# Layer one's gMLP first half, last two token chunks: block pairs as seven half products

## The chip, the cores and the metric

The kernel runs on one core of one Trainium2 chip. The metric is the device time of one execution in microseconds (us), and the numbers given are medians of several executions.

The engines have short names in the text: PE is the matrix engine (TensorE), DVE is VectorE, ACT is ScalarE, POOL is GpSimd, and SP is SyncE, which only issues transfers (DMAs). Each engine takes its instructions in the order in which the program lists them; an instruction that waits holds up all that stand behind it on that engine.

## The reference

Two layers, each made of an attention block with a linear kernel and a gMLP block, over 2048 tokens of 512 features, in 32-bit floats:

```python
for layer in range(2):
    x = x + attention(layernorm(x), wqkv, wo)      # 32 heads of 16, phi(t) = elu(t) + 1
    z = gelu(layernorm(x) @ w_in)                  # 2048 x 1792
    z1 = z[:, :896]; z2 = layernorm(z[:, 896:])
    g = w_sp @ z2 + b_sp[:, None]                  # over the tokens: 2048 x 2048
    x = x + (z1 * g) @ w_out
```

The change concerns `z1 = gelu(layernorm(x) @ w_in[:, :896])` of the first of the two layers. The kernel calls the layers L = 0 and L = 1, so "layer one" is L = 0.

## The kernel before

Every 32-bit operand of a product is split into a high part h (rounded to the matrix engine's format) and a low part l, and a product is three matmuls, h·h, h·l and l·h (`mm3`, L227). An ACT copy makes h (L214) and a DVE subtraction makes l (L217).

The tokens are cut into 16 tiles of 128 (i) and 4 chunks of 512 (n), the 896 features of z1 into 7 blocks of 128 (f). For each layer the phases are P1 (keys and queries), a transition, P2 (attention output, both gMLP input products) and P4 (the product over the tokens, the gate and the output product).

P2 of layer L = 0 is `P2.run`, a loop over token steps s = 1 to 18. The order within a step is written out by hand, and each engine's queue is in that order; nothing is scheduled afterwards. A step between 6 and 15 holds, for different tiles at once:

- `b(s)`: the turned attention input of tile s is read back from a scratch tensor (qt), turned on DVE (L448) and split (ACT L214, DVE L217).
- `c(s-1)`: the attention output product of tile s-1, 12 matmuls of 512 columns. `c2` adds it to x on DVE (L907) and takes mean and variance (L359, L361 on DVE; L363, L364, L366 on POOL). `c3` normalises on ACT (L372), stores x, and stores the tile through a scratch tensor (yt) so that it can be read back turned.
- `d(s-2)`: tile s-2 comes back from yt, is turned on DVE (L448) and split (ACT L214, DVE L217) into its 128 columns of xT[n].
- `e4(s-4)`: the last layernorm of z2 for tile s-4, on ACT (L372).
- `e(s-3)`: the z2 product of tile s-3, 24 matmuls of 448 columns, into two banks; `e2` is its gelu on ACT (L1068), `e3` its statistics on DVE and POOL.
- twice `f()`: one block (n, f) of z1 for one chunk, 12 matmuls of 512 columns; `fout` is its gelu on ACT (L1135) and its store (tensor z). Blocks are queued as soon as a chunk's four tiles are done, at the end of steps 5, 9, 13 and 17.
- `sums.tick()`: sums of the weights of the later product over the tokens (POOL L1604, loads and stores on SP).

Fourteen of the 28 blocks are thus worked off up to step 13 and nine more in steps 14 to 18; the five that are left when the loop ends run in `P4.run`, in the `while p2.f()` loop, beside the splits for P4's first products.

Layer L = 1 already computes chunks 2 and 3 by blocks 0 to 2 and 3 to 5 as seven products (`first_a`, `first_b`, `T1`, `T2`, `tail`). `first_a(f)` does half a product into bank u, and ACT copies u to bank y (L1170); `first_b(f)` then adds the other half to u itself. In layer L = 1 other work stands between the two (`odd`, L1190 and on). The weight sums that this needs are made in the P1 phase of L = 1 from the raw weights, on POOL (`FSums.sums`), split on ACT and DVE, and stored to a scratch tensor (w1s).

PSUM has 8 banks; a bank is free again when its reader on ACT or DVE is done.

Of the kernel before, what the change touches and what calls it, by code (L numbers as in the profile page):

```python
# [15 lines left out]
P = 128  # L16
# [95 lines left out]
WADD = {2: 0, 4: 1, 6: 2}  # L112
# [40 lines left out]
def mixer_kernel(ctx: ExitStack, tc: tile.TileContext, x_in, wqkv, wo_d, win1_d, win2_d, wsp_d, bsp_d, wout_d,  # L153
# [299 lines left out]
    class P1:  # L453
# [185 lines left out]
        def run(self, sums):  # L639
            side = deque([self.win2] * NF)  # L640
            ND = NT - DEFER
            for s in range(1, NT + 2):
# [54 lines left out]
                if self.L:  # L697
                    if 9 <= s < NT + 1:
                        sums.halve(28 + (s - 9) // 2, None, (s - 9) % 2)
                    if s in WADD:  # L700
                        if not WADD[s]:
                            self.fsums = FSums()
                        self.fsums.load(WADD[s])
                    if s - 1 in WADD:
                        self.fsums.sums(WADD[s - 1])
                    if s - 2 in WADD:
                        self.fsums.split(WADD[s - 2])
                        if WADD[s - 2] == 2:
                            self.fsums.close()
# [15 lines left out]
    class FSums:  # L725


        def __init__(self):
            self.raw = quads.get([P, 2, 2, 512])
            self.parts = quads.get([P, 2, 2, 512], F32R)  # L730

        def load(self, f):
            for k in range(2):
                nc.sync.dma_start(self.raw[:, f % 2, k], win1_d[f + 3 * k])

        def sums(self, f):
            p, q = (self.raw[:, f % 2, k].rearrange("p (k n) -> p k n", k=2) for k in range(2))
            for o, a, b, op in ((q[:, 1], q[:, 0], q[:, 1], OP.add), (q[:, 0], p[:, 0], q[:, 0], OP.subtract),
                                (p[:, 0], q[:, 1], p[:, 0], OP.subtract), (p[:, 1], p[:, 1], p[:, 0], OP.subtract)):
                nc.gpsimd.tensor_tensor(o, a, b, op=op)  # L740

        def split(self, f):
            p, q = (self.raw[:, f % 2, k].rearrange("p (k n) -> p k n", k=2) for k in range(2))
            for m in range(2):
                h, l = (self.parts[:, m, k] for k in range(2))
# [4 lines left out]
                for k in range(2):  # L750
                    nc.sync.dma_start(w1sums[f, m][k], self.parts[:, m, k].bitcast(F32))

        def close(self):
            quads.put(self.raw, self.parts)
# [72 lines left out]
    class P2:  # L827
        def __init__(self, p1):
# [4 lines left out]
            self.wf = deque([w1parts[f] for f in list(range(NF)) * 2 + [0, 6, 1, 2, 6]]  # L833
# [107 lines left out]
        def d_low(self, i):  # L941
# [9 lines left out]
            if k == 3:  # L951
                self.fnext = [(n, f) for f in (range(NF) if n < 2 or not self.L else (NF - 1,))]
# [226 lines left out]
        def first_out(self, *fs):  # L1179
            for f in fs:  # L1180
                if f:
                    self.wfetch()
# [1229 lines left out]
```

## Time and profile before

| | |
|---|---|
| median of 3 runs | 1346.25 us (1345.23 to 1347.37) |
| span of the profiled execution | 1345.0 us, from its first instruction to its last |
| its own time | recorded as the span alone; the fastest of the runs lies 0.2 us above it, the median 1.25 us |
| mean granted TensorE clock | 0.999 |
| PE busy | 1338.2 us, 99% of the span |
| DVE, ACT, POOL busy | 1043.7, 726.6, 462.6 us (78%, 54%, 34%) |
| HBM read and written | 204.08 and 101.71 MB |

PE's busy time comes from matmuls whose ends are modelled, so a matmul of 512 columns shows some 389 ns while the next one starts after some 227. Durations on PE are therefore taken from start to start. A row of a timeline gives start, duration, engine, line, what it writes and reads, how many instructions are merged into it, and in brackets how long the engine idled before it and for what.

### The profile page before, as it was taken

How to read it: one execution, taken by the hardware profiler on the slowest of the kernel's cores; microseconds unless marked ns; L12 is line 12 of the kernel's file. 1: busy time of each engine (PE TensorE's matmuls, PEld its weight loads, DVE VectorE, ACT ScalarE, POOL GpSimd, SP SyncE). 2: the span in 40 equal slices, each digit the busy share in tenths (PEclk: the TensorE clock that was granted, in tenths of full speed). 3: DMA queues.
4: the chain of work that ended last, by engine and by line, in shares of the span. 5: the costliest groups of instructions: out<-in, count | busy, mean ns of one | idle time of the engine just before them, and what ended most of it. 6: DMA issues, size and time to landing. Idle time of an engine off the chain costs nothing.

```text
span 1345.0 us, 19202 instructions
## 1 busy us (share of the span) xinstructions
PE 1338.2 (99%) x6538; PEld 1141.4 (85%) x6538; DVE 1043.7 (78%) x1662; ACT 726.6 (54%) x1219; POOL 462.6 (34%) x613
## 2 busy tenths in 40 slices
PE   9999999999999999999999999999999999999998
PEld 7888888888888888889988888888888888888898
DVE  7679877763797789888867777778689858899885
ACT  5774534334643264445677755557677433666454
POOL 3755675544022300301425543544531012121021
PEclk9999999999999999999999999999999999999999
DMA  5897477877877986884867652678777445579343
GB/s 184 279 318 272 164 262 254 293 270 258 298 236 256 285 265 203 293 306 80 179 172 230 173 133 89 208 238 272 217 206 231 168 168 178 177 241 313 122 79 64
DMA packets 172403, 290.30 MB, mean 216 GB/s; under 512 B 14480, under 2 KB 53904, under 8 KB 172048
## 3 DMA queue, kind: packets, MB, share of 16 engines
q1 hardware_dynamic: 154192, 251.58, 55.5%
q0 software_dynamic: 18112, 37.49, 13.0%
q8 instruction: 51, 0.84, 0.2%
q14 instruction: 48, 0.39, 0.1%
HBM read 204.08 MB, written 101.71 MB: 227 GB/s over the span
## 4 chain that ended last, share of the span: by engine, by line
PE 96%; DMA 1%; DVE 1%; ACT 1%; SPq 0%; issue 0%; POOL 0%; DVEq 0%
PE bank L228 14%; PE bank L230 14%; PE bank L229 13%; PE bank L1920 12%; PE bank L1921 12%; PE bank L1922 12%; PE bank L2118 3%; PE bank L2119 3%; PE bank L2120 3%; PE bank L986 1%; PE bank L988 1%; PE bank L987 1%; DMA pg<-yt 1%; PE bank L384 1%; PE bank L2132 1%; PE bank L2131 1%
## 5 line engine op out<-in xcount | busy, mean ns | idle before, releaser
L1921 PE MATMUL bank<-qd,pg 128*128 128x512 f32 x736 | 286.5, 389 | 0.0
L1920 PE MATMUL bank<-qd,pg 128*128 128x512 f32 x736 | 286.4, 389 | 0.0
L1922 PE MATMUL bank<-qd,pg 128*128 128x512 f32 x736 | 286.3, 389 | 0.0
L1695 ACT ACTIVATE qd<-qd 128x1024 fp32r<-128x1024 f32 x142 | 149.4, 1053 | 127.3 <-PE bank L1922 107.0
L1698 DVE TENSOR_TENSOR qd<-qd,qd 128x1024 fp32r<-128x1024 f32 x132 | 169.2, 1284 | 52.6 <-ACT qd L1695 41.7
L230 PE MATMUL bank<-qd,pg 128*128 128x512 f32 x448 | 174.6, 390 | 0.0
L1921 PEld LDWEIGHTS bank<-qd,pg 128*128 128x128 f32 x736 | 138.2, 188 | 28.9 <-DVE qd L1698 0.3
L1920 PEld LDWEIGHTS bank<-qd,pg 128*128 128x128 f32 x736 | 138.2, 188 | 28.7 <-DVE bg L1870 0.2
L1922 PEld LDWEIGHTS bank<-qd,pg 128*128 128x128 f32 x736 | 138.2, 188 | 28.7
L228 PE MATMUL bank<-qd,pg 128*128 128x512 f32 x308 | 120.6, 392 | 0.3 <-DVE pg L217 0.3
L1961 POOL TENSOR_TENSOR bg<-bg,pg 128x512 f32<-128x512 f32 x28 | 45.7, 1632 | 218.1 <-ACT qd L1695 99.4
L229 PE MATMUL bank<-qd,pg 128*128 128x512 f32 x308 | 120.1, 390 | 0.0
L230 PEld LDWEIGHTS bank<-qd,pg 128*128 128x128 f32 x448 | 84.1, 188 | 17.8 <-DVE pg L217 0.2
L363 POOL TENSOR_SCALAR rs<-mv 128x1 f32<-128x1 f32 x80 | 25.1, 314 | 190.0 <-DVE mv L361 181.0
L372 ACT ACTIVATE pg<-pg,nb,rs 128x512 f32<-128x512 f32 x52 | 42.2, 812 | 85.5 <-POOL nb L366 79.3
L1604 POOL TENSOR_TENSOR pg<-pg,pg 128x512 f32<-128x512 f32 x48 | 68.0, 1417 | 59.2 <-DMA pg<-in_wsp_dram 57.3
L214 ACT ACTIVATE pg<-pg 128x512 fp32r<-128x512 f32 x85 | 53.0, 624 | 61.7 <-DVE pg L1789 18.4
L2120 PE MATMUL bank<-wo,qd 128*128 128x256 f32 x288 | 81.4, 283 | 0.0
L2118 PE MATMUL bank<-wo,qd 128*128 128x256 f32 x276 | 78.2, 283 | 0.0
L2119 PE MATMUL bank<-wo,qd 128*128 128x256 f32 x276 | 78.0, 283 | 0.0
L228 PEld LDWEIGHTS bank<-qd,pg 128*128 128x128 f32 x308 | 57.9, 188 | 12.5 <-DVE pg L217 0.7
L229 PEld LDWEIGHTS bank<-qd,pg 128*128 128x128 f32 x308 | 58.0, 188 | 12.1 <-DVE qd L217 0.2
(276 smaller groups left out, 3278.6 us busy)
## 6 DMA issues: line engine op xcount, KB each, us to landing
qd<-s SPq DMA_DIRECT2D x62, 512.0 KB, 4.2
qd<-in_wsp_dram SPq DMA_DIRECT2D x40, 512.0 KB, 4.1
qd<-hP SPq DMA_DIRECT2D x40, 512.0 KB, 4.7
pg<-z SPq DMA_DIRECT2D x56, 256.0 KB, 4.9
pg<-in_wsp_dram SPq DMA_DIRECT2D x52, 256.0 KB, 4.3
s<-pg SPq DMA_DIRECT2D x48, 256.0 KB, 3.7
z<-pg SPq DMA_DIRECT2D x40, 256.0 KB, 3.3
pg<-w POOLq DMA_DIRECT2D x38, 256.0 KB, 4.6
```

The source lines that it names most:

```text
L228: nc.tensor.matmul(out, ah, bh, start=start, stop=False)
L229: nc.tensor.matmul(out, ah, bl, start=False, stop=False)
L230: nc.tensor.matmul(out, al, bh, start=False, stop=stop)
L1604: nc.gpsimd.tensor_tensor(t, a, b, op=OP.add)
L1695: self.mark = nc.scalar.activation(w[:, 0], r, AF.Copy)
L1698: nc.vector.tensor_sub(w[:, 1], r, w[:, 0].bitcast(F32))
L1920: m(out, h[:, o], w[:, 0, j, :], start=start, stop=False, skip_group_check=True)
L1921: m(out, h[:, o], w[:, 1, j, :], start=False, stop=False, skip_group_check=True)
L1922: m(out, l[:, o], w[:, 0, j, :], start=False, stop=stop, skip_group_check=True)
L2118: m(out, A, x, start=start and f == 0, stop=False, skip_group_check=True)
L2119: m(out, A, y, start=False, stop=False, skip_group_check=True)
L2120: m(out, B, x, start=False, stop=stop and f == 2, skip_group_check=True)
```

## The change

Layer L = 0 gets the same scheme for chunks 2 and 3, blocks 0 to 5; block 6 of both chunks, and chunks 0 and 1, stay as they were. For a pair of blocks (f, f+3) and the two chunks, four blocks of 12 matmuls become seven products of 6.

- In the loop, `FONE` says how many plain blocks a step does: 2 in steps 6, 7, 8 and 10, 11, 12, and 1 in steps 9, 13 and 14, none later. Steps 15, 16 and 17 each end with `first_a(f)`, `first_b(f)` and `first_out(f)` for f = 0, 1, 2, directly one behind the other.
- The weight sums move from L = 1's P1 to these token steps. Steps 13, 14 and 15 load two raw weight tiles each (SP); steps 14, 15 and 16 make four sums (now on DVE, 128x256 each), four high parts (ACT) and four low parts (DVE), and store four tiles of 256 KB (SP). The stores also serve L = 1, whose POOL sums, loads and stores go.
- Step 16 ends with `raw(0)` (DVE, 128x1024). Step 17 gets `T1` (two DVE subtractions of 128x1024), `T1split` (ACT and DVE, 128x1024) and `raw(1)`, right behind `d(15)` and ahead of `e4` and `e2`. Step 18 gets `T2`, eight DVE operations of 128x512, and two weight loads on POOL's queue.
- The loop over the five remaining blocks in `P4.run` is replaced by `tail()` for both layers: one plain block and the other five products of each pair, 102 matmuls, with the splits of P4's first products at three places in it.
- From tile 5 on, normalised and turned tiles live in the z tiles in place of pages.

PE loses 18 matmuls (6400 rows become 6382), DVE and ACT gain rows, and SP loses eight.

The diff, cut to its core:

```diff
+FONE = {6: 2, 7: 2, 8: 2, 9: 1, 10: 2, 11: 2, 12: 2, 13: 1, 14: 1}
-WADD = {2: 0, 4: 1, 6: 2}
+WADD = {13: 0, 14: 1, 15: 2}
...
         def load(self, f):
-            for k in range(2):
-                nc.sync.dma_start(self.raw[:, f % 2, k], win1_d[f + 3 * k])
+            self.raw[f] = [load(win1_d[f + 3 * k]) for k in range(2)]
...
         def split(self, f):
+            raw = self.raw.pop(f)
+            p, q = (t.rearrange("p (k n) -> p k n", k=2) for t in raw)
+            V = nc.vector
+            V.tensor_add(q[:, 1], q[:, 0], q[:, 1])
+            V.tensor_sub(q[:, 0], p[:, 0], q[:, 0])
+            V.tensor_sub(p[:, 0], q[:, 1], p[:, 0])
+            V.tensor_sub(p[:, 1], p[:, 1], p[:, 0])
             for m in range(2):
-                h, l = (self.parts[:, m, k] for k in range(2))
+                h, l = pages.get(PAGE, F32R), pages.get(PAGE, F32R)
                 for k, s in enumerate((q[:, 1 - m], p[:, m])):
                     high(h[:, 256 * k:256 * k + 256], s)
                 for k, s in enumerate((q[:, 1 - m], p[:, m])):
                     low(l[:, 256 * k:256 * k + 256], s, h[:, 256 * k:256 * k + 256])
...
+                if s == NT + 1:
+                    self.T1()
+                    self.T1split()
+                    self.raw(1)
+                if s == NT + 2:
+                    quads.put(*self.xT.pop(2))
+                    self.T2()
+                    self.wfetch()
+                    self.wfetch()
                 if s >= 4:
                     self.e4(s - 4)
                 self.xturn.load(s - 1)
                 if s >= 3:
                     self.e(s - 3)
                     self.e2(s - 3)
                     self.e3(s - 3)
-                self.f()
-                self.f()
+                for _ in range(FONE.get(s, 0)):
+                    self.f()
+                if s in (15, 16, 17):
+                    self.first_a(s - 15)
+                    self.first_b(s - 15)
+                    self.first_out(s - 15)
+                if s in WADD:
+                    if not WADD[s]:
+                        self.fsums = FSums()
+                    self.fsums.load(WADD[s])
+                if s - 1 in WADD:
+                    self.fsums.split(WADD[s - 1])
...
-            while p2.f():
-                self.zahead(min(self.zmade, 3))
+            for _ in p2.tail():
+                n += 1
+                if n == 1:
+                    self.sums.store()
+                self.zahead(n - 1)
+                self.sp(n - 1)
+                if n < 3:
+                    self.fetch(n + 3)
             self.zahead(3)
-            if p2.win1 is not None:
-                p2.win1.free()
```

Three places in the queues. The words in brackets name whose count an instruction waits for (a DMA queue, an engine); lines 200 to 700 move by one in the changed kernel, later ones by others.

ACT around step 15, before. The rows are the split for b(15), the normalisation of tile 14, the split for d(13), e4(11), the two gelus of e(12), and the gelus of two plain blocks:

```order
L214 ACTIVATE pg_351_3365<-pg_350_3363 128x512 [waits DMAHW7_49,DVE_49]
L372 ACTIVATE pg_353_3393<-pg_327_3115,nb,rs 128x4x4x32 [waits DVE_49,DMAHW3_49,Activation_49,Pool_49]
L214 ACTIVATE qd_16_3275<-pg_354_3397 128x4x128 [waits DVE_49]
L372 ACTIVATE z_z_3308<-z_z_3308,nb,rs 128x896 [waits Activation_49]
L1068 ACTIVATE z_z_3430<-bank_127_3404 128x448 [waits PE_49]
L1068 ACTIVATE z_z_3430<-bank_128_3417 128x448 [waits PE_49]
L1135 ACTIVATE pg_356_3456<-bank_129_3443 128x512 [waits DMAHW5_49,PE_49,Activation_49]
L1135 ACTIVATE pg_357_3473<-bank_130_3460 128x512 [waits DMAHW6_49,PE_49,Activation_49]
```

ACT at the same place in the changed kernel, from the four high parts of the first weight sums on:

```order
L215 ACTIVATE pg_324_3350<-pg_312_3225 128x256 [waits DMAHW3_49,DMAHW2_49,DVE_49]
L215 ACTIVATE pg_324_3350<-pg_311_3223 128x256 [waits DMAHW1_49,DVE_49]
L215 ACTIVATE pg_326_3358<-pg_312_3225 128x256 [waits DMAHW7_49]
L215 ACTIVATE pg_326_3358<-pg_311_3223 128x256 [waits DVE_49]
L215 ACTIVATE z_q<-pg_329_3374 128x512 [waits DVE_49]
L373 ACTIVATE z_y<-pg_305_3115,nb,rs 128x4x4x32 [waits DVE_49,Activation_49,Pool_49]
L215 ACTIVATE qd_16_3279<-z_y 128x4x128 [waits DVE_49]
L373 ACTIVATE z_z_3312<-z_z_3312,nb,rs 128x896 [waits Activation_49]
L1059 ACTIVATE z_z_3441<-bank_126_3415 128x448 [waits PE_49]
L1059 ACTIVATE z_z_3441<-bank_127_3428 128x448 [waits PE_49]
L1161 ACTIVATE bank_128_3454<-bank_129_3455 128x512 [waits PE_49]
L1134 ACTIVATE pg_332_3469<-bank_129_3455 128x512 [waits PE_49,Activation_49]
```

Four high parts have come ahead of step 15's own rows, and behind the gelus of e(12) the copy of u to y (L1161) stands before the gelu of u.

PE at the end of step 15 in the changed kernel (the last three rows of `first_a(0)`, the first of `first_b(0)` and what follows it):

```order
L1144 MATMUL bank_129_3455<-qd_14_2753,bg_5_1763 128x512
L1145 MATMUL bank_129_3455<-qd_15_2754,bg_5_1763 128x512
L1146 MATMUL bank_129_3455<-qd_14_2753,bg_6_1764 128x512
L1144 MATMUL bank_129_3455<-qd_14_2753,bg_5_1763 128x512 [waits Activation_49]
L1145 MATMUL bank_129_3455<-qd_15_2754,bg_5_1763 128x512
L1146 MATMUL bank_129_3455<-qd_14_2753,bg_6_1764 128x512
```

The seventh matmul writes the bank that the copy reads, and waits for ACT; in the kernel before, two plain blocks stood here.

DVE at the turn from step 16 to step 17, before (the split of d(14), the statistics of z2 of tile 13, the turn and the split of d(15), and the statistics of tile 14):

```order
L217 TENSOR_TENSOR qd_17_3276<-pg_362_3517,qd_16_3275 128x4x128 [waits Activation_49]
L359 BN_STATS st<-z_z_3550 128x6 [waits Activation_49] x2
L361 BN_AGGR mv<-st 128x2 [waits DVE_49,Pool_49]
L448 STREAM_TRANSPOSE pg_367_3603<-pg_363_3522 128x4x128 [waits DMAHW5_49,DMAHW2_49]
L217 TENSOR_TENSOR qd_17_3276<-pg_367_3603,qd_16_3275 128x4x128 [waits Activation_49]
L359 BN_STATS st<-z_z_3634 128x6 [waits Activation_49] x2
```

and in the changed kernel, from the last low part of the weight sums on:

```order
L218 TENSOR_TENSOR pg_347_3615<-pg_333_3473,pg_346_3614 128x256 [waits Activation_49]
L1151 TENSOR_TENSOR qd_18_3622<-qd_14_2753,qd_15_2754 128x1024
L449 STREAM_TRANSPOSE z_y<-pg_342_3542 128x4x128 [waits DMAHW6_49,DMAHW5_49]
L218 TENSOR_TENSOR qd_17_3280<-z_y,qd_16_3279 128x4x128 [waits Activation_49]
L1185 TENSOR_TENSOR qd_18_3622<-qd_16_3279,qd_18_3622 128x1024
L1186 TENSOR_TENSOR qd_18_3622<-qd_18_3622,qd_17_3280 128x1024 [waits DVE_49]
L218 TENSOR_TENSOR qd_19_3636<-qd_18_3622,qd_19_3636 128x1024 [waits Activation_49]
L1151 TENSOR_TENSOR qd_18_3622<-qd_14_2753,qd_15_2754 128x1024
L360 BN_STATS st<-z_z_3667 128x6 [waits Activation_49] x2
```

`raw(0)`, `T1` (L1185, L1186), the low part of T1 and `raw(1)` have come in between. On ACT, the high part of T1 stands between the split of d(15) and e4(13), and the copy of u to y for f = 2 behind the gelus of e(14).

115 lines of the change are left out of this document (52 added, 63 removed).

## The prediction

> **What bounds the kernel now.** I read the page first (busy time, the chain that ended last), then what PE waited for, then the timelines of layer L = 0's last token steps. On the page, the row of busy time and the head of the chain:
>
> ```profile
> PE 1338.2 (99%) x6538; PEld 1141.4 (85%) x6538; DVE 1043.7 (78%) x1662; ACT 726.6 (54%) x1219; POOL 462.6 (34%) x613
> ...
> PE 96%; DMA 1%; DVE 1%; ACT 1%; SPq 0%; issue 0%; POOL 0%; DVEq 0%
> ```
>
> and all the waits of PE's matmuls in the execution:
>
> ```profile
> PE bank L617 <- DVE pg L612: 2.3, 1, 2.3
> PE bank L1153 <- ACT bank L1170: 0.4, 1, 0.4
> PE bank L228 <- DVE pg L217: 0.3, 1, 0.3
> ```
>
> PE is the bound and waits 3 us in all. So a matmul taken away is worth its full spacing, and a wait put in front of PE is lost in full. The stage that changes, by the first matmul of each block on PE (step 15 begins at 292.34, step 16 at 305.39, step 17 at 318.45, P4's first product at 349.99):
>
> ```profile
> 292.34 0.39 PE L228 MATMUL bank<-qd,pg 128*128 128x512 f32 x1
> ...
> 295.06 0.36 PE L228 MATMUL bank<-bg,qd 128*128 128x448 f32 x1
> ...
> 299.92 0.39 PE L228 MATMUL bank<-qd,bg 128*128 128x512 f32 x1
> ...
> 305.39 0.39 PE L228 MATMUL bank<-qd,pg 128*128 128x512 f32 x1
> ...
> 308.11 0.36 PE L228 MATMUL bank<-bg,qd 128*128 128x448 f32 x1
> ...
> 312.98 0.39 PE L228 MATMUL bank<-qd,bg 128*128 128x512 f32 x1
> ...
> 318.45 0.36 PE L228 MATMUL bank<-bg,qd 128*128 128x448 f32 x1
> ...
> 323.31 0.39 PE L228 MATMUL bank<-qd,bg 128*128 128x512 f32 x1
> ...
> 326.06 0.36 PE L228 MATMUL bank<-bg,qd 128*128 128x448 f32 x1
> ...
> 330.92 0.39 PE L228 MATMUL bank<-qd,bg 128*128 128x512 f32 x1
> ...
> 349.99 0.39 PE L1920 MATMUL bank<-qd,pg 128*128 128x512 f32 x1
> ```
>
> The last seven plain blocks are 84 matmuls from 330.92 to 349.99: 0.227 us each, 2.72 us for twelve, 1.36 for six. An e of 24 is 4.87 us (308.11 to 312.98). PE never pauses, though ACT is late. ACT in steps 15 and 16 and at the end of 17:
>
> ```profile
> 301.79 0.82 ACT L372 ACTIVATE pg<-pg,nb,rs 128x512 f32<-128x512 f32 x1 [3.78 <-POOL nb L366]
> ...
> 304.06 0.95 ACT L1068 ACTIVATE z_z<-bank 128x448 f32<-128x448 f32 x2
> ...
> 311.47 0.82 ACT L372 ACTIVATE pg<-pg,nb,rs 128x512 f32<-128x512 f32 x1 [5.24 <-POOL nb L366]
> ...
> 313.75 0.94 ACT L1068 ACTIVATE z_z<-bank 128x448 f32<-128x448 f32 x2
> ...
> 323.74 0.63 ACT L214 ACTIVATE qd<-pg 128x512 fp32r<-128x512 f32 x1 [4.50 <-DVE pg L448]
> ...
> 324.28 1.12 ACT L372 ACTIVATE z_z<-z_z,nb,rs 128x896 f32<-128x896 f32 x1
> ...
> 325.31 0.96 ACT L1068 ACTIVATE z_z<-bank 128x448 f32<-128x448 f32 x2
> ```
>
> The gelus of e(12), whose matmuls ended at 299.92, are done at 305.01; those of e(14), ended at 323.31, at 326.27. Before, this lateness costs nothing: the banks that it holds are not asked for again so soon. That is what the change spends.
>
> **Part 1: matmuls removed.** 18 at 0.227: **-4.1 us**, certain.
>
> **Part 2: the copy between the halves.** The seventh matmul of each of the three new blocks waits for ACT's copy of u, which stands behind the gelus of e. Step 14 loses one plain block, so c(14) would start 2.72 earlier, at 289.62, and e(12) at 292.34. Its low part comes from DVE:
>
> ```profile
> 292.44 0.69 DVE L217 TENSOR_TENSOR qd<-pg,qd 128x512 fp32r<-128x512 f32 x1 [1.84 <-ACT qd L214]
> ...
> 296.25 1.09 DVE L448 STREAM_TRANSPOSE pg<-pg 128x512 f32<-128x512 f32 x1 [0.90 <-DMA pg<-qt]
> ...
> 298.66 0.68 DVE L907 TENSOR_TENSOR pg<-pg,bank 128x512 f32<-128x512 f32 x1
> ...
> 322.60 1.10 DVE L448 STREAM_TRANSPOSE pg<-pg 128x512 f32<-128x512 f32 x1 [6.84 <-DMA pg<-yt]
> ```
>
> It is there at 293.13, while e(12)'s third matmul would run at 292.75: a wait of **0.4**. So e(12) ends at 297.6 and the first half of block 0 at 299.0. The chain that leads to the copy is not paced by PE: c2(14) on DVE ran at 298.66, long after c(14) had ended at 295.06, because it stands behind b(15)'s turn at 296.25, which waited for the qt load. Statistics, POOL, L372 at 301.79, and so on to 305.01 follow. Nothing there can come earlier in the changed kernel; with the copy's duration,
>
> ```profile
> L1170 ACT ACTIVATE bank<-bank 128x512 f32<-128x512 f32 x3 | 1.7, 583 | 0.0
> ...
> L1807 DVE TENSOR_TENSOR pg<-z_z,pg 128x256 fp32r<-128x256 f32 x40 | 15.1, 418 | 1.8 <-ACT pg L1803 1.8
> ...
> L1160 DVE TENSOR_TENSOR qd<-qd,qd 128x1024 f32<-128x1024 f32 x2 | 2.4, 1218 | 0.0
> ...
> L1695 ACT ACTIVATE qd<-qd 128x1024 fp32r<-128x1024 f32 x142 | 149.4, 1053 | 127.3 <-PE bank L1922 107.0 <-issue 9.2 <-DMA qd<-in_wsp_dram 5.0
> ```
>
> it ends at 305.6 at the earliest: a wait of 6.6 as the lower bound. The weight sums push it further. At the end of step 14 they put eight DVE instructions of 128x256 (0.42 each, 3.4 in all) ahead of b(15)'s turn, where DVE had 0.9 free; the chain moves by about 2.6. **First wait: 9.2** (6.6 to 9.2); PE goes on at 308.2, and c(15) starts at 309.6, against 305.39 before.
>
> Step 16: c(15) ends at 312.3, e(13) at 317.2, the first half at 318.6. In the kernel before, the gelus of e(13) end 6.6 behind the end of c(15) (314.69 against 308.11); with the copy 7.2, so 319.5. **Second wait: 0.9.** It could vanish, or with the weight sums of step 15 be 2.
>
> **Part 3: T1 in front of the gelus of e(14).** In step 17, e(14) runs to 325.8 and the first half of block 2 to 327.1. ACT must first do the split of d(15), which follows c(15) through yt; before, its turn started at 322.60, 14.5 behind the end of c(15), now at 326.8. From the turn's start to the end of d(15)'s low part before: 2.5 (the ACT part ends at 324.37, a low part takes 0.69). Then, new, T1 on DVE, two of 1.22, and its high part on ACT, 1.05; then e4 1.12, gelus 0.96, copy 0.58. 326.8 + 2.5 + 2.4 + 1.05 + 1.12 + 0.96 + 0.58 = 335.4. **Third wait: 8.4.** The way through yt sets its bounds. Its rows for tiles 14 and 15:
>
> ```profile
> 303.75 0.65 SPq L419 DMA_DIRECT2D yt<-pg  x1
> ...
> 307.71 0.32 SPq L196 DMA_DIRECT2D pg<-yt  x1
> ...
> 313.71 1.18 SPq L419 DMA_DIRECT2D yt<-pg  x1
> ...
> 319.79 0.32 SPq L196 DMA_DIRECT2D pg<-yt  x1
> ```
>
> Store to load took 4.0 and 6.1: the third wait is 2.1 shorter if tile 15 goes as tile 14 went (6.3). It is longer if the 12 stores and 6 loads of the weight sums, of 256 KB each, slow the way: in 270 to 345 us the transfers are busy 80% of the time,
>
> ```profile
> 270.00:345.00 75.00, 8.73 (x8) 1.00 0.80 269
> ```
>
> at 269 GB/s (the last two columns), and 18 x 256 KB = 4.7 MB is 17 us of transfers at that rate, over about 55 us. I take twice the same 2.1 as the upper bound, 12.6. SP's queue also gets four stores and two loads more in a step ahead of the yt store.
>
> **Part 4: the tail.** e(15), then 102 matmuls (23.2 us) in place of 84. Their operands need T2 (eight DVE operations), which has the time of e(15) and four blocks, 11.7 us; the high parts of T6 stand behind e4(15) on ACT. Adding e(15)'s gelus, statistics and POOL, they are ready within about half a microsecond of PE: **0.5**, up to 2.5, since POOL has four sums of L1604 and four weight loads ahead of e4(15)'s statistics. The splits for P4 have 72 matmuls of cover. In L = 1 the sums, loads and stores that go ran beside PE without a wait: 0.
>
> **Part 5: the clock.** After PE's last matmul the granted clock falls, and the first eight matmuls are slow (columns of the first two rows: length, busy and count by engine, PE first, then clock):
>
> ```profile
> 1340.00:1342.00 2.00, 1.18 (x10) 0.98 (x8) 0.75 (x2) 0.00 (x0) 0.00 (x0) 1.00 0.40 135
> 1342.00:1345.00 3.00, 0.00 (x0) 0.00 (x0) 0.00 (x0) 0.00 (x0) 0.00 (x0) 0.68 0.26 87
> ...
> 2.31 3.78 PE L617 MATMUL bank<-pg,ones 128*128 128x512 f32 x8 [2.31 <-DVE pg L612]
> 5.90 1.08 PE L384 MATMUL bank<-ident,pg 128*128 128x128 f32 x4
> ```
>
> PE ends at 1341.2; a mean of 0.68 over 1342 to 1345 is half the clock for 1.9 us, so it fell within about 2 us of idling. At the start eight matmuls took 3.59 us, 0.449 each, twice 0.227: 1.8 us lost on the way to full clock. Two waits of over 8 us would each cost that: **+3.5** (0 to 3.6).
>
> The Trainium skill (TensorE: Matmul & The Clock Gate, section "HAM oscillation — how this bites in real kernels") speaks against this change: leave no gap on PE longer than about 3.4 us, or it restarts at half rate. By its window of 3.4 us at half rate each long wait costs 1.7 us more, an estimate, and the sum would have +3.4 in place of +3.5; without the rule it would be 3.5 lower. This kernel has no gap in mid-run that could test it.
>
> **The sum**: -4.1 + 0.4 + 9.2 + 0.9 + 8.4 + 0.5 + 3.5 = +18.8 on a span of 1345.0, so 1363.8. The median of the runs lies 1.25 above that span, which gives 1365. In the median's terms I say **1364 us**, one less, since a PE at half clock may hide a little of the second wait. Lower bounds: -4.1 + 0.4 + 6.6 + 0 + 6.3 + 0 + 0 = +9.2, 1355.5. Upper: -4.1 + 0.4 + 9.2 + 2 + 12.6 + 2.5 + 3.6 = +26.2, 1372.5.
>
> **Rivals.**
> - *The gain stays.* The copies meet an ACT that is free, and each block loses only the copy, 0.6: -4.1 + 1.8 = -2.3, 1344; without any wait 1342. For it: in L = 1 the same copy cost PE 0.4 us. Against: there other work stands between the halves, here none does, and ACT is 5.1 and 3.0 us late on e before the change. It decides for this if the copy of block 0 ends before 299. Chance 6%.
> - *Even.* One wait only, of the size of the gain. 4%.
> - *One long wait.* Tile 15 gets back before PE needs it, the first wait stays: -4.1 + 0.4 + 9.2 + 1.8 = +7.3, 1353.5. Against: T1 and the yt way alone fill 8 us. 11%.
> - *The transfers decide.* The added 4.7 MB stretch qt and yt ways in steps 14 to 17 and the weight loads of the tail, and each long wait grows by 4 or more: 1373 and over. For it: the 80%. Against: the loop itself is slower then, and the rate lower. 14%.
> - *The change does not do what it says*: PE's rows fall by 18, so no.
>
> **How the numbers follow.** The forecast with its bounds has 65%, and is the likeliest. The range 1354 to 1373 takes it in and a part of its neighbours, about 80%. This kernel's measurement tells 0.2% (2.7 us) from no change: faster 6%, same 4%, slower 90%.
>
> **What would show it.** Right: PE waits for L1161 (the copy) in two long stretches and one short, 16 to 20 us in all, near 299 and 327; the granted clock below 1 just behind them; P4's first product near 369; from there on the same spacing as before. Wrong: no wait of PE on L1161 above 1 us (part 2), a third wait under 5 or over 13 (part 3), a granted clock of 1.00 in both places (part 5), or a difference that arises behind 370 us, in L = 0's P4 or in L = 1, of which I expect nothing.

## The result and the profile after

The changed kernel takes 1378.41 us (median of 4 runs, 1377.44 to 1378.9), the one before 1345.97 beside it: a ratio of 1.0234 with an interval of 1.0222 to 1.0247, 32.4 us slower. The profiled execution has a span of 1377.1 us, 32.1 more than that of before.

The row of busy time on the page, and the head of the chain that ended last:

```profile
PE 1339.7 (97%) x6520; PEld 1140.3 (83%) x6520; DVE 1075.0 (78%) x1700; ACT 735.1 (53%) x1234; POOL 462.1 (34%) x615
...
PE 70%; DMA 2%; DVE 2%; POOL 1%; ACT 1%; issue 0%; SPq 0%; DVEq 0%; POOLq 0%; ACTq 0%
```

PE has 18 matmuls less and is busy as long as before; the time went into waits. All waits of its matmuls above 0.4 us (in total, how often, the longest):

```profile
PE bank L1144 <- ACT bank L1161: 28.3, 3, 18.5
PE bank L618 <- DVE pg L613: 2.3, 1, 2.3
PE bank L1144 <- ACT bg L215: 1.0, 1, 1.0
PE bank L1145 <- DVE bg L218: 0.9, 1, 0.9
```

The copy of u (L1161) is waited for three times, as forecast, but for 28.3 us. Where, and what PE does behind each wait, in its timeline:

```profile
297.86 0.40 PE L1146 MATMUL bank<-qd,bg 128*128 128x512 f32 x1
316.80 0.80 PE L1144 MATMUL bank<-qd,bg 128*128 128x512 f32 x1 [18.55 <-ACT bank L1161]
317.39 0.63 PE L1145 MATMUL bank<-qd,bg 128*128 128x512 f32 x1
...
337.35 0.40 PE L1146 MATMUL bank<-qd,bg 128*128 128x512 f32 x1
346.53 0.80 PE L1144 MATMUL bank<-qd,bg 128*128 128x512 f32 x1 [8.79 <-ACT bank L1161]
...
361.37 0.39 PE L1146 MATMUL bank<-qd,pg 128*128 128x512 f32 x1
362.76 0.50 PE L1144 MATMUL bank<-bg,pg 128*128 128x512 f32 x1 [1.00 <-ACT bg L215]
364.21 0.75 PE L1145 MATMUL bank<-bg,pg 128*128 128x512 f32 x1 [0.95 <-DVE bg L218]
364.76 0.63 PE L1146 MATMUL bank<-bg,pg 128*128 128x512 f32 x1
...
382.75 0.39 PE L1951 MATMUL bank<-qd,pg 128*128 128x512 f32 x1
```

The first row of a pair is the last matmul of the first half, the second the first of the second half. Take from start to start, less the usual spacing: 18.7 us lost in step 15, 9.0 in step 17, 1.1 in step 16 (at 328.48), and 1.16 and 1.22 in the tail, where PE waits for T6 (the split sums that T2 prepares for the tail's products); a further 0.55 at 372.74 is a wait for the load of a stored weight sum. Behind the two long waits and behind the pair in the tail the next matmuls start 0.43 apart (0.37 where they have 448 columns), nearly twice the usual. The windows around these places (columns: length, busy time and count of PE, PEld, DVE, ACT and POOL, then PE's clock):

```profile
317.00:321.00 4.00, 4.00 (x12) 3.19 (x13) 1.97 (x7) 1.17 (x4) 3.25 (x5) 0.64 0.24 70
...
347.00:351.00 4.00, 4.00 (x12) 3.25 (x12) 3.86 (x9) 0.68 (x2) 2.85 (x4) 0.55 0.00 0
...
361.00:368.00 7.00, 5.05 (x15) 3.46 (x14) 5.05 (x7) 5.73 (x10) 3.64 (x5) 0.76 1.02 316
```

The three slow spells lose 1.5, 2.0 and 1.7 us, from the spacing of their matmuls. P4's first product (382.75) starts 32.8 us later than before (349.99), and the span is 32.1 us longer: all that comes behind it, L = 1 included, makes a difference of only 0.7 us.

**What is late in step 15.** DVE, from the low parts of the first weight sums on:

```profile
299.06 0.76 DVE L218 TENSOR_TENSOR pg<-pg,pg 128x256 fp32r<-128x256 f32 x2 [3.44 <-DMA x<-pg]
303.36 1.08 DVE L449 STREAM_TRANSPOSE pg<-pg 128x512 f32<-128x512 f32 x1 [3.54 <-DMA z<-pg]
309.30 0.69 DVE L218 TENSOR_TENSOR pg<-pg,z_q 128x512 fp32r<-128x512 f32 x1 [4.87 <-DMA w1s<-pg]
309.91 0.68 DVE L898 TENSOR_TENSOR pg<-pg,bank 128x512 f32<-128x512 f32 x1
```

A page is one of the 22 tiles of 128x512 that the kernel hands out and takes back. Three times DVE wants to write a page whose old content is still being stored (to x, z and w1s): 11.9 us. The last row is c2(14), with which the chain to the copy begins; it ran at 298.66 before. SP's queue shows when the stores were issued:

```profile
293.06 0.66 SPq L904 DMA_DIRECT2D x<-pg  x1
294.01 0.37 SPq L420 DMA_DIRECT2D yt<-z_y  x1
299.69 0.32 SPq L197 DMA_DIRECT2D pg<-yt  x1
300.42 0.32 SPq L1129 DMA_DIRECT2D z<-pg  x1
...
301.83 2.63 SPq L740 DMA_DIRECT2D w1s<-pg  x4
```

The x store was issued in time and took 5.9 us to land. The z store stands behind the read-back of yt, which is issued 5.7 us behind the yt store because it waits for that to land, and the four stores of the weight sums stand behind the z store. The z store was not even issued when DVE got there (299.8). ACT then does what the prediction listed: normalisation at 313.05, gelus of e(12) from 315.31, the copy at 316.16.

### The profile page after: what moved, and what is told of

Its sections match the earlier page's. It is cut to its first block, busy times and chain, and to the rows that moved or that the text cites. A ratio compares the mean times of both kernels' runs of the same rounds, so it can differ in the third digit from the quotient of the medians.

```text
span 1377.1 us, 19226 instructions
## 1 busy us (share of the span) xinstructions
PE 1339.7 (97%) x6520; PEld 1140.3 (83%) x6520; DVE 1075.0 (78%) x1700; ACT 735.1 (53%) x1234; POOL 462.1 (34%) x615
## 3 DMA queue, kind: packets, MB, share of 16 engines
q0 software_dynamic: 19616, 41.17, 13.7%
## 4 chain that ended last, share of the span: by engine, by line
PE 70%; DMA 2%; DVE 2%; POOL 1%; ACT 1%; issue 0%; SPq 0%; DVEq 0%; POOLq 0%; ACTq 0%
PE bank L1951 12%; PE bank L1953 12%; PE bank L1952 12%; PE bank L229 6%; PE bank L230 6%; PE bank L231 6%; PE bank L2149 3%; PE bank L2150 3%; PE bank L2151 3%; PE bank L977 1%; PE bank L978 1%; PE bank L979 1%; PE bank L1146 1%; PE bank L1144 1%; PE bank L1145 1%; DMA qd<-hP 1%
## 5 line engine op out<-in xcount | busy, mean ns | idle before, releaser
L1951 PE MATMUL bank<-qd,pg 128*128 128x512 f32 x736 | 286.5, 389 | 0.3 <-DVE bg L1901 0.3
L1953 PE MATMUL bank<-qd,pg 128*128 128x512 f32 x736 | 286.4, 389 | 0.0
L1952 PE MATMUL bank<-qd,pg 128*128 128x512 f32 x736 | 286.4, 389 | 0.0
L1729 DVE TENSOR_TENSOR qd<-qd,qd 128x1024 fp32r<-128x1024 f32 x132 | 165.9, 1258 | 46.2 <-ACT qd L1726 44.6
L231 PE MATMUL bank<-qd,pg 128*128 128x512 f32 x448 | 174.7, 390 | 0.0
L1951 PEld LDWEIGHTS bank<-qd,pg 128*128 128x128 f32 x736 | 138.2, 188 | 29.2 <-DVE bg L1901 0.7
L1953 PEld LDWEIGHTS bank<-qd,pg 128*128 128x128 f32 x736 | 138.2, 188 | 28.8 <-DVE pg L1791 0.2
L1952 PEld LDWEIGHTS bank<-qd,pg 128*128 128x128 f32 x736 | 138.2, 188 | 28.7
L229 PE MATMUL bank<-qd,pg 128*128 128x512 f32 x264 | 103.2, 391 | 0.4 <-ACT pg L215 0.2
L230 PE MATMUL bank<-qd,pg 128*128 128x512 f32 x264 | 102.9, 390 | 0.0
L231 PEld LDWEIGHTS bank<-qd,pg 128*128 128x128 f32 x448 | 84.1, 188 | 18.3 <-DVE pg L218 0.4
L1635 POOL TENSOR_TENSOR pg<-pg,pg 128x512 f32<-128x512 f32 x48 | 68.1, 1419 | 50.1 <-DMA pg<-in_wsp_dram 48.0
L215 ACT ACTIVATE pg<-pg 128x512 fp32r<-128x512 f32 (+1 forms) x86 | 50.0, 592 | 40.9 <-DVE pg L1820 19.4
L218 DVE TENSOR_TENSOR pg<-pg,pg 128x512 fp32r<-128x512 f32 (+1 forms) x84 | 58.0, 698 | 9.0 <-ACT pg L215 5.2
L543 POOL TENSOR_TENSOR pg<-pg,pg 128x512 f32<-128x512 f32 x30 | 39.9, 1331 | 58.3 <-DVE pg L537 56.4
L229 PE MATMUL bank<-bg,qd 128*128 128x448 f32 x160 | 59.3, 371 | 0.0
```

The lines of the kernel that those rows point to most:

```text
L229: nc.tensor.matmul(out, ah, bh, start=start, stop=False)
L230: nc.tensor.matmul(out, ah, bl, start=False, stop=False)
L231: nc.tensor.matmul(out, al, bh, start=False, stop=stop)
L1635: nc.gpsimd.tensor_tensor(t, a, b, op=OP.add)
L1729: nc.vector.tensor_sub(w[:, 1], r, w[:, 0].bitcast(F32))
L1951: m(out, h[:, o], w[:, 0, j, :], start=start, stop=False, skip_group_check=True)
```

## The experiments

All ran beside the kernel before; each ratio is to it. **Theory A**: PE loses what the halves wait for the copy; the copy is late through the chain of tile 14, through DVE's work on the weight sums and through pages in flight. **Rivals**: that chain alone (B), the transfers (C), DVE's work alone (D).

### No weight sums

```diff
-            self.raw[f] = [load(win1_d[f + 3 * k]) for k in range(2)]
+            self.kept.append([load_r(t, PAGE) for t in w1parts[f]])
...
         def split(self, f):
+            pass
```

> The weight sums are left out: no raw loads, no 12 sums, high and low parts, no stores; the halves of the seven products take the stored plain weights instead (six tiles loaded on POOL's queue), so z1 of chunks 2 and 3 is wrong. PE's instructions are the same as in the changed kernel. Theory A (the first wait of 18.7 us is a page wait: DVE stands in front of tiles whose old content is still being stored, 11.9 us in three waits, because the sums take pages and put stores in the queues): the first wait on the copy L1161 falls to 6 to 8 us, the second stays near 1 and the third near 9, the tail's waits of 1.2 + 1.2 shrink; 1363 to 1367 us. Rival B (the wait is the chain c2, c3, gelu, copy itself, whatever DVE does): 1376 or more. Rival C (the traffic of the sums slows all transfers): like A, but the third wait also shrinks to 6 or less and yt's store-to-load time with it; under 1362.

Measured: 1363.46 us, ratio 1.0123 (1.0108 to 1.0138), 15 us of the 32 gone. The PE waits (the line numbers are 19 lower here):

```profile
PE bank L1125 <- ACT bank L1142: 12.3, 3, 7.0
```

The first wait is 7.0, the chain's own part, as theory A has it, and B falls. But the third fell too, from 8.8 to 4.7, and with it the way of tile 15 through yt: from its store to the load that reads it back took 3.6 us, against 6.4 in the changed kernel. Both are what C had foreseen and A had not; only C's time, under 1362, is missed, by 1.5 us, so this run alone does not refute C. In the changed kernel two things reach d(15)'s turn together: the sums of step 16, which stand ahead of it on DVE, and the read-back from yt, for which DVE waits 0.36 us more,

```profile
332.51 4.15 DVE L218 TENSOR_TENSOR pg<-pg,pg 128x256 fp32r<-128x256 f32 x4 [0.48 <-ACT pg L215]
338.16 1.08 DVE L449 STREAM_TRANSPOSE z_y<-pg 128x512 f32<-128x512 f32 x1 [0.36 <-DMA pg<-yt]
```

and here DVE waits 2.63 us at that place for yt alone:

```profile
323.28 1.10 DVE L449 STREAM_TRANSPOSE z_y<-pg 128x512 f32<-128x512 f32 x1 [2.63 <-DMA pg<-yt]
```

The run without a transfer, below, tells the two apart.

### Sums made, not stored

```diff
-                for k, t in enumerate((h, l)):
-                    nc.sync.dma_start(w1sums[f, m][k], t.bitcast(F32))
```

> The sums are made as in the changed kernel, on DVE and ACT and in the same pages, but their 12 stores of 256 KB are left out, and the tail and layer L = 1 read plain weights in place of the sums (wrong z1 there). Theory A (pages held by stores in flight): DVE's wait of 4.9 us for the w1s stores goes, the waits for x and z (3.4 and 3.5 us) stay; the first wait is 12 to 15 us, 1372 to 1375 us. Theory A2 (the pages are short however they are used, the stores only name the wait): some other store takes the place, first wait 17 or more, 1377 or more. Rival D (DVE's time for the sums, 3.4 us a step, is all of it): no change, 1377 or more. Rival C (traffic): first wait under 10, third under 7.

Measured: 1376.02 us, 1.0215 (1.0199 to 1.023). DVE in step 15, and PE's first wait:

```profile
298.57 0.76 DVE L218 TENSOR_TENSOR pg<-pg,pg 128x256 fp32r<-128x256 f32 x2 [2.55 <-DMA x<-pg]
302.88 1.08 DVE L449 STREAM_TRANSPOSE pg<-pg 128x512 f32<-128x512 f32 x1 [3.54 <-DMA z<-pg]
304.65 0.69 DVE L218 TENSOR_TENSOR pg<-pg,z_q 128x512 fp32r<-128x512 f32 x1 [0.70 <-ACT z_q L215]
...
312.15 0.79 PE L1142 MATMUL bank<-qd,bg 128*128 128x512 f32 x1 [13.48 <-ACT bank L1159]
```

As A says: the wait for w1s is gone, those for x and z stay, and the first wait is 13.5; C (first wait under 10, third under 7, measured 8.4) and D (no change) do not fit. The median is 1 us above A's range. The profiled execution is the fastest of the four (1373.91) and lies within it, so its rows do not explain that microsecond; in its tail the waits add up to 4.0 us, where the changed kernel has 2.9, 2.3 of them for a load of plain weights.

### The same sums without a transfer

```diff
-            raw = self.raw.pop(f)
+            raw = [pages.get(PAGE) for _ in range(2)]
+            for t, k in zip(raw, (0, 3)):
+                h, l = held(f + k)
+                nc.vector.tensor_add(t, h.bitcast(F32), l.bitcast(F32))
...
+                self.kept[m, f] = [h, l]
```

> The weight sums are made in the same steps 14 to 16 and on the same engines as in the changed kernel, but without any transfer: the raw weights are the sums of the high and low parts that layer L = 0 holds anyway (two DVE additions of 128x512 more for each f, some 1.2 us), and all six pairs stay in pages until the tail. Layer L = 1 makes its own sums in its P1, as in the kernel before. The result is the same. Theory A (of the first wait's 18.7 us, 7.1 are the chain, some 3 the DVE work of the sums, and the rest DVE's waits for tiles whose stores are under way): the waits of DVE for x, z and w1s stores in step 15 (3.4, 3.5 and 4.9 us) go, the first wait is 9.5 to 11, the third 5.5 to 8; 1366 to 1370 us. Rival D (DVE's work on the sums is what costs, the stores only stand beside it): first wait 14 or more, 1374 or more. Rival P (pages are as short with 12 kept, whatever is stored): DVE still waits 5 us or more for x or z stores, first wait 13 or more.

Measured: 1375.08 us, 1.0204 (1.0187 to 1.0221). DVE and POOL in step 14:

```profile
297.45 0.43 DVE L742 TENSOR_TENSOR pg<-pg,pg 128x256 f32<-128x256 f32 x1
297.92 1.40 DVE L743 TENSOR_TENSOR pg<-pg 128x256 f32<-128x256 f32 x1
...
301.65 1.06 DVE L450 STREAM_TRANSPOSE pg<-pg 128x512 f32<-128x512 f32 x1
...
297.52 2.93 POOL L1668 TENSOR_TENSOR pg<-pg,pg 128x512 f32<-128x512 f32 x2
```

No wait for a store is left in step 15. The first wait is 11.8 by PE's starts, 0.8 above A's range: b(15)'s turn comes at 301.65 in place of 296.06 in the run without sums, since the sums take 6.4 us (from 295.26), where eight operations of 0.42 and two of 0.62 would be 4.6. While POOL adds, an operation of 0.43 takes 1.40. Rival P (first wait 13 or more) and D (14 or more) do not fit, though D's time (1374 or more) does. The time does not follow the first wait, which A had wrong. With twelve pages kept, T2 waits 4.6 us for a page in the tail, and the third wait stays at 9.2: tile 15's read-back is issued at 324.08, 2.3 us behind its store, but DVE, at work without a pause from 325.10, comes to d(15)'s turn only at 333.23.

```profile
329.66 2.52 DVE L219 TENSOR_TENSOR pg<-pg,pg 128x256 fp32r<-128x256 f32 x4
332.10 1.21 DVE L1189 TENSOR_TENSOR qd<-qd,qd 128x1024 f32<-128x1024 f32 x1
333.23 1.07 DVE L450 STREAM_TRANSPOSE z_y<-pg 128x512 f32<-128x512 f32 x1
```

For the third wait, then, DVE's work on the sums is enough, without any traffic of theirs. Of the 9.2, 1.2 are the two additions that only this run has; the run without stores, where DVE does not wait for yt at this place either, has 8.4.

So the first wait, by differences of start-to-start times of one profile each, is put together thus: the chain 7.1; DVE's work on the sums 3.5 (11.8 less 7.1, less the 1.2 of two additions that only this run has); loads and pages in flight, which no run separates, 3.1 (up to the 13.7 without stores); the stores of the sums 5.0 (up to 18.7). The tail experiment below, which leaves step 15 alone, had 17.0, so a part is good to about 2 us.

### Sums made elsewhere

In P1 of L = 0 (POOL, quads, as L = 1 did before), and in token steps 7 to 12:

```diff
-WADD = {13: 0, 14: 1, 15: 2}
+WADD = {2: 0, 4: 1, 6: 2}      (P1 of L = 0)
+WADD = {7: 0, 9: 1, 11: 2}     (token steps)
```

> The weight sums are made in the P1 phase of layer L = 0, as the kernel before made them in that of L = 1 (sums on POOL, in two free quads, no pages; loads in steps 2, 4 and 6), and the tail loads all six pairs back; the order in steps 15 to 17 is that of the changed kernel. The result is the same. Theory A: what the run without sums won (15 us) is won here too with the sums still made, as long as P1 hides them: first wait 6 to 8, third 4 to 6, 1362 to 1366 us. Rival C (the traffic costs time wherever it is: at 40 to 100 us the transfers are busy 89 to 97% of the time): P1 of L = 0 gets 3 us or more longer, 1367 or more.

> The only edit: the weight sums move to token steps 7 to 12 (loads in 7, 9 and 11, sums and splits one step later, on DVE as in the changed kernel), all 12 stored tiles give their pages back at once, and the tail loads six pairs in place of three. The order of steps 15 to 17 stays. The result is the same. Theory A (the late steps are short of pages, and DVE waits there for tiles whose store is under way): with six pages more free and no stores of sums in steps 14 to 16 the first wait falls from 18.7 to 6.5 to 8, the third to 5 to 9; the earlier steps, where PE has 2 us more work each, hide the sums; 1362 to 1367 us. Rival C (the traffic costs wherever it is, as the 11 us in P1 of L = 0 showed): new waits of PE in steps 8 to 13, together 4 us or more; 1368 or more.

Measured: 1378.62 us, 1.0234 (1.0208 to 1.026), and 1380.46 us, 1.025 (1.0235 to 1.0266): rival C both times. The first wait fell to 8.6 and 6.2, but the sums cost as much where they now are. P1 of L = 0 in the first, the changed kernel's row ahead of it:

```profile
40.00:60.00 20.00, 20.00 (x89) 16.49 (x89) 14.03 (x23) 14.48 (x25) 14.80 (x15) 1.00 0.89 303
```

```profile
40.00:60.00 20.00, 17.41 (x71) 14.02 (x70) 13.02 (x22) 11.65 (x22) 15.28 (x20) 0.91 0.92 309
```

PE, never idle there before, loses 10 us by the end of P1. In the second, PE waits in steps 10 to 14, up to 3.7 us at once. In both the sums come with their transfers and with work on POOL or DVE; which of these costs the 10 us in P1, or the waits in steps 10 to 14, was not separated.

### Only the order

```diff
                         self.c(s - 1)
+                        if s in (15, 16):
+                            self.first_a(s - 15)
                         self.c2(s - 1)
...
-                    self.first_a(s - 15)
                     self.first_b(s - 15)
                     self.first_out(s - 15)
+                if s == NT + 1:
+                    self.T1()
+                    self.T1split()
+                    self.raw(1)
```

> first_a of the three blocks moves away from first_b: right behind c(s-1), so that ACT copies u before the gelus of e; in step 17 it stands ahead of d(15), and T1, its split and raw(1) move behind first_out. The sums stay. Theory A (each half waits for its copy behind ACT's late chain; the first wait is doubled by DVE): PE no longer waits for the copy L1161 by more than 1.5 us anywhere, the third wait falls from 9 to under 6 and is now for d(15) or for T1's work in the tail. But DVE is still stopped by pages for 11.9 us, so PE waits instead for c(15), b(15) or e(13)'s operand in step 15 or 16, by about 10 to 16 us; 1362 to 1374 us. Rival B (only the order matters): 1345 or less. Rival E (the order doesn't matter, everything waits for DVE): 1377 or more.

> Both edits at once: the weight sums are left out (plain weights in their place, so z1 of chunks 2 and 3 is wrong) and first_a stands right behind c(s-1), with T1, its split and raw(1) behind first_out of step 17. Theory A (order and late DVE each cost; together they are the whole loss): the wait of 7.1 us in step 15 that the run without sums still had goes below 1, the one of 4.8 in step 17 goes or becomes a wait of 1 to 4 for d(15), and with them their half-clock spells; what stays is a wait for T6 in the tail, 4 to 9 us, since T1, T2 and e4(15) now stand later (8.7 in the run with only the order changed). 1348 to 1356 us. Rival (the chain through c2, c3 and yt is too slow for PE whatever the order of the halves): 1360 or more, with PE waiting for d(14) and d(15).

Measured: 1377.2 us, 1.0226 (1.0209 to 1.0243) with the sums, 1364.75 us, 1.013 (1.0112 to 1.0149) without. Both miss theory A, the second by 9 us, and both times lie where a rival had them: E (1377 or more) for the first, the slow chain (1360 or more) for the second. In the first the copy is still waited for, 7.6 us: ahead of it on ACT stands the split of b(15), which needs the turn that waits for the z store. In the second PE waits 2.5 us for d(14) and 1.4 for d(15), as that rival says, but its largest wait is in the tail. There both runs lose part of what the steps win. The row in the run with sums, on ACT:

```profile
359.80 1.13 ACT L373 ACTIVATE z_z<-z_z,nb,rs 128x896 f32<-128x896 f32 x1 [13.00 <-POOL nb L367]
```

e4(15) waits for tile 15's statistics. POOL makes the last part of them and had itself waited 3.7 us for DVE, where T1, `raw(1)` and T2 now stand later, beside POOL's sums. T6's high parts stand behind e4(15), and PE waits 8.5 us for T6 (9.7 in the run without sums).

### Only the tail

```diff
-                if s == NT + 2:
-                    sums.tick()
...
-            self.e4(NT - 1)
...
+                if r == 7 and not L:
+                    self.T2b()
...
+                if self.L == 0 and n < 3:
+                    self.sums.tick(n < 2)
```

> Only the tail is edited: POOL's four sums for the later product leave step 18 and run inside the tail, e4(15) moves behind the split of T4, T6 is split ahead of the last four subtractions of T2. The halves and the weight sums stay as in the changed kernel. The result is the same. Theory F (in the tail PE waits for T6 because T2's 128x512 subtractions take 1.8 us in place of 0.65 while POOL's sums run, and e4(15) with them): T2's eight take under 6 us, the waits of 1.2 and 1.2 for T6 and the half-clock spell behind them go, 3 to 4.5 us faster than the changed kernel, 1374 to 1375.5. Rival: the tail waits for e(15) or T7 in their place, under 1 us of difference.

Measured: 1376.54 us, 1.0226 (1.0204 to 1.0249). The waits for T6 and the third slow spell are gone, as theory F says; two waits of 0.9 and 1.0 us come at P4's first products (388.84 and 390.00), and the intervals do not tell it from the changed kernel, so the 3 to 4.5 us are not shown. What the changed kernel's tail waits for, on ACT, POOL and DVE:

```profile
361.05 1.14 ACT L373 ACTIVATE z_z<-z_z,nb,rs 128x896 f32<-128x896 f32 x1 [5.54 <-POOL nb L367]
...
351.49 6.09 POOL L1635 TENSOR_TENSOR pg<-pg,pg 128x512 f32<-128x512 f32 x4
...
350.87 0.69 DVE L1202 TENSOR_TENSOR pg<-pg,qd 128x512 f32<-128x512 f32 x1
351.48 1.88 DVE L1201 TENSOR_TENSOR pg<-pg,qd 128x512 f32<-128x512 f32 x1
```

These four sums and four weight loads on POOL stand ahead of tile 15's statistics. Beside the sums a DVE subtraction takes 1.88 in place of 0.69; with the sums moved, T2's last four took 0.7 each.

### PE kept busy in the waits

```diff
+                    if s != 16:
+                        b = banks.get(PAGE)
+                        for _ in range(78 if s == 15 else 36):
+                            nc.tensor.matmul(b, self.A[s - 15][0][:, 0:P], ...)
+                        banks.put(b)
                     self.first_b(s - 15)
```

> Between first_a and first_b PE gets matmuls into a spare bank that nobody reads: 78 in step 15 (17.7 us at 0.227) and 36 in step 17 (8.2 us), so it is busy for nearly all of the first and the third wait. The result is the same. Clock theory (after each long wait some eight matmuls run at half rate, 1.9 us lost each): the granted clock stays at 1.00 at both places, the two spells go, 3 to 4 us faster than the changed kernel (1374 to 1375.5), and the third spell in the tail stays. Rival (the matmuls behind a wait are slow for another reason, or the next wait takes what is won): within 1 us of the changed kernel.

```profile
317.00:321.00 4.00, 4.00 (x20) 3.40 (x19) 2.31 (x5) 1.82 (x5) 2.29 (x2) 1.00 0.42 133
...
347.00:351.00 4.00, 4.00 (x21) 3.68 (x20) 3.97 (x5) 1.80 (x3) 3.80 (x5) 1.00 0.17 66
```

Measured: 1379.32 us, 1.0242 (1.0223 to 1.026), runs from 1376.1 to 1382.1. The clock is 1.00 behind both waits, where it was 0.64 and 0.55, so idling is what lowers it. But the profiled execution, the fastest of the four, is only 2.7 us shorter than that of the changed kernel, as the tail's wait for T6 grows from 1.2 to 3.0, and in the median nothing is won: the next wait takes it, as the rival says.

### All edits together

The order, the tail, b(15) read back a step earlier, and block 6 of chunk 2 moved. First the sums in P1 with the order and e4(15) alone, and the same with the moved block:

```diff
-FONE = {6: 2, 7: 2, 8: 2, 9: 1, 10: 2, 11: 2, 12: 2, 13: 1, 14: 1}
+FONE = {6: 2, 7: 2, 8: 2, 9: 1, 10: 2, 11: 2, 12: 2, 13: 1}
...
                 if s == NT + 2:
+                    self.f()
```

> The sums in P1 of L = 0 as above, first_a right behind c(s-1), T1 behind first_out, and e4(15) moved out of ACT's queue ahead of T6 and T7 to behind the split of T4. The result is the same. Theory A: only waits of 0 to 3 us for d(15) and 0 to 3 in the tail are left; with 18 matmuls fewer (-4.1) it ends at 1342 to 1349 us. Rival (seven products are not worth it in this place: the chain from c(15) over yt to d(15), T2 and T6 is longer than the work PE has left): 1350 or more, with a wait of over 5 us for d(15) or T6.

> As the kernel above, and the one plain block of step 14, block 6 of chunk 2, moves to the start of step 18, ahead of e(15), so that PE has 2.7 us more to do while d(15) comes back. The result is the same. Theory A: a wait for d(15) shrinks by up to 2.7 us, and if step 14 without it makes PE wait for d(12) or b(14), by as much there: 1341 to 1348 us, 0 to 2.7 below the kernel above. Rival: the wait only moves to step 14, no difference.

Measured: 1371.3 us, 1.0182 (1.0161 to 1.0203), and 1372.56 us, 1.019 (1.0168 to 1.0212). About 10 us of each are P1's. In the first PE loses 2.4 us to d(15) and 5.3 to T6's low part (T2 beside POOL's sums), so theory A is out, and the rival's wait and time (1350 or more, even without P1's 10 us) are met. The moved block takes the wait for d(15) away and puts one of 3.8 for the copy into step 15: the wait only moves, as the rival says, though not to step 14.

Then everything, with the sums in steps 7 to 12, and without sums:

```diff
-                self.qturn.load(s + 1)
+                if s != NT - 2:
+                    self.qturn.load(s + 1)
...
                 self.xturn.load(s - 1)
+                if s == NT - 3:
+                    self.qturn.load(NT - 1)
```

> All edits together: the weight sums in steps 7 to 12, first_a right behind c(s-1) and T1 behind first_out, the tail as in the run with only the tail edited, the read-back of b(15) asked for one step earlier (ahead of what SP waits for), and block 6 of chunk 2 in step 18 instead of 14. The result is the same. Theory A: no wait over 2 us is left in steps 13 to 18 and the tail, so the 18 matmuls come through: 1342 to 1349 us. Rival (the chain from c(15) over yt to d(15), T2 and T6 is longer than PE's work): a wait of 4 us or more for d(15) or T6, 1350 or more.

> The lower bound of the scheme in this place: no weight sums at all (plain weights in their place, so z1 of chunks 2 and 3 is wrong), with every edit of the order: first_a behind c(s-1), T1 behind first_out, the tail with POOL's sums and e4(15) moved and T6 first, b(15) read back earlier, block 6 of chunk 2 in step 18. Theory A (waits in order, each with its own cause, and all of them curable but for the work of the sums): waits of 1 to 2 us each for d(14) and d(15), none over 2 in the tail; 1343 to 1349 us, even with the kernel before or some us faster. Rival (the chain c(15), yt, d(15), T1, T2, T6 is longer than the work that PE has left, in any order): a wait of 4 us or more in steps 17 to the tail, 1351 or more, so that the scheme can't win here however the sums are made.

Measured: 1372.0 us, 1.0189 (1.0171 to 1.0207), and 1359.61 us, 1.0089 (1.0074 to 1.0104). With the sums, PE waits 4.4 us for b(13) in step 14, several times for d, and 3.8 us for weights in the tail; theory A misses by over 20 us, and the rival has the time but not the place. Without any, what is left:

```profile
PE bank L229 <- ACT qd L215: 5.2, 3, 2.8
PE bank L1125 <- ACT bank L1239: 2.9, 1, 2.9
...
PE bank L1126 <- DVE bg L218: 1.3, 1, 1.3
```

No copy of the first halves is waited for; PE waits for d(12), d(13) and d(14), then in the tail. The time is the rival's, 12.0 us above the kernel before; its single wait of 4 us or more did not appear, the loss is spread. None of the orders tried gives a version that beats the kernel before, with the sums or without.

## Why the prediction was wrong

The direction was right, and so was the outline of the mechanism: two long waits and a short one for the copy, and half the clock behind the long ones. The time (1364, range to 1373) was 14 us short. By its steps, as lost by PE's starts:

| step | predicted | measured |
|---|---|---|
| part 1, 18 matmuls | -4.1 | -4.1 |
| part 2, wait for d(12) | 0.4 | none |
| part 2, first wait | 9.2 (6.6 to 9.2) | 18.7 |
| part 2, second wait | 0.9 (0 to 2) | 1.1 |
| part 3, third wait | 8.4 (6.3 to 12.6) | 9.0 |
| part 4, tail | 0.5 (up to 2.5) | 2.9 |
| part 5, clock | 3.5 (two spells) | 5.2 (three) |
| sum | 18.8 | 32.8 (span: 32.1) |

**The step that failed is "First wait: 9.2".** Its base, the chain paced by the qt load, was right: 6.6 forecast, 7.1 in the run without sums. On top of it the prediction put 2.6 for eight DVE instructions at 0.42. The runs show about 3.5 for that work, since DVE runs beside POOL's sums, and 8.1 more for loads, pages in flight and stores. The bound "6.6 to 9.2" was no upper bound: it held DVE's work and nothing of the pages it writes. The queue listing already gave the high parts of these sums waits on DMA queues; I priced the operations and no such wait. The rival that the transfers decide (14%) has the time (1373 and over) by another mechanism: it let the ways through qt and yt stretch and each long wait grow by 4 or more. The third grew by 0.6, and the way through yt took 5.7, 2.3 and 6.4 us for tiles 13 to 15 against 4.3, 4.0 and 6.1 before. The loss is in one place, where DVE catches up with the stores that SP issues.

Part 3 had the size right (8.4; its own terms give 8.3), partly by luck. The path that it lists, yt and T1, is the one on which d(15)'s turn ends its waiting. But it had left the sums of step 16 out of this wait: they stand ahead of the turn, end 0.36 us before the read-back, and give 8.4 and 9.2 by themselves in the two runs above in which DVE does not wait for yt there, while without them and with a quicker way through yt the wait is 4.8. Part 4 named e4(15) behind POOL's sums and loads, which is what the rows show, and took 0.5 where its own upper end, 2.5, was close to the 2.4 for T6. Part 5 had the two spells right in kind (1.5 and 2.0 against 1.8 each) and missed the third. That behind P4's first product next to nothing changes was right (0.7 us).

## What to carry to other kernels

When instructions are added to an engine's queue, price the tile that each one writes as well as its operation: find who last held it, when that store is issued, and what stands ahead of it on the issuing queue. A saving on the bounding engine is worth taking only if the engines that feed it keep their distance; here PE saved 4.1 us and came up against three chains that had been hidden by the work removed. A step's upper bound has to hold the waits that the queue listing names, not only the work.

## What the runs showed of the hardware that was not expected

The clock fell in the tail after two waits that lost 1.16 and 1.22 us with one matmul between them (0.43 per matmul behind them), while the single one of 1.12 us in step 16 left it at full speed. In the other runs a single gap that lost 2.28 us left it at 1.00 (sums not stored, in the tail, at 368.87), and one that lost 2.45 lowered it (order alone without sums, 0.64 in 316 to 317 us). The Trainium skill (TensorE: Matmul & The Clock Gate, section "HAM oscillation — how this bites in real kernels") warns of gaps longer than about 3.4 us; here shorter ones were enough. Where the boundary lies is known no better than by these rows.

DVE operations with two operands in SBUF slow down beside operations of that kind on POOL: in the changed kernel 31 single 128x512 additions and subtractions that overlap a 128x512 operation of POOL on two tensors take 1.24 us in the mean and up to 1.88, the 170 others 0.68 (counted over the timeline). Those that read one operand from a PSUM bank are not slowed: 25 that overlap take 0.68 in the mean, as do the 80 that don't. The Trainium skill (SBUF — State Buffer, section "Who interferes with whom") says that an operation with two inputs in SBUF contends with one on GpSimd that reads SBUF; this trace agrees.
